# Two loads issued ahead of four stores, and ScalarE's order changed, in a chunked-attention and rational-MLP kernel

## The chip, the cores and the metric

The kernel runs as one program on one core of a Trainium2 chip. Its time is the device time of one execution in microseconds (us); of the kernel before it is the median of three executions. A profile of one more execution shows every instruction of the five engines: TensorE (PE, with its weight loads as PEld), VectorE (DVE), ScalarE (ACT), GpSimd (POOL) and SyncE (SP, which issues nearly all DMAs here). One DMA moves one block of a tensor between HBM and SBUF, and SP issues its DMAs one after the other.

## The reference

Attention over chunks of 64 rows, and then a two-layer MLP whose activation is a rational function (numpy, cut):

```python
scores = (1 / sqrt(64)) * q_c @ k_c.T          # per batch, head and chunk of 64 rows
attn = exp(scores - max); attn = attn / (sum(attn) + 1e-9)
x = (attn @ v_c) -> [4608 tokens, 512]         # heads side by side
h = x @ w_in                                   # 512 -> 2048
P = a[0] + a[1]*h + a[2]*h*h + a[3]*h*h*h
Q = 1 + |b[0]|*|h| + |b[1]|*h*h
out = (P / (Q + 1e-6)) @ w_out                 # 2048 -> 512, float32
```

## The kernel before

The 4608 tokens are 18 blocks of 256 (numbers 0 to 17). Each block has four steps s = 0 to 3, one for each 512 columns of the hidden layer. To keep float32 accuracy each operand of a matmul is split into a high part (`hi`, a cast) and a low part (`lo`, what the cast lost), and a product is three matmuls: hi*hi, hi*lo, lo*hi.

Every instruction is placed by hand. `START` lists the first 12 steps; after that `step(g)` walks a string of letters for each step, and each letter issues its instructions into the in-order queues of the engines. So the order of two letters matters only where they share an engine, or where they take a buffer from the same pool tag. The strings are `EARLY` (blocks 3 and 4), `STEADY` (blocks 5 to 16) and `LAST` (block 17). The letters that matter here, in block n:

- `F f` (PE): the hidden layer's matmuls into `ph`. `c a` (ACT): `C` and `A` read from `ph` (L402, L386). `Q p P` (DVE, L410, L422, L426), `b I J` (ACT, L391, L414, L418) and `g H R` (DVE, L431, L435, L439 in steps 0 and 1, L501, L505, L509 in steps 2 and 3) make the rational function. `Gp` (POOL, L444) makes its low part, in steps 0 and 1.
- `Z z y` (PE): the output matmuls of the step two before. For steps 2 and 3 of a block a seven-product scheme stands in their place, done in the next block: `V` (PE) in steps 0 and 1 and `V2` (PE) in step 1 add into `xacc` and `po`. Their sums are split by `hb` (ACT, L549, the high parts `shi`) and `lb` (DVE, L553, the low parts `slo`); `s0 h0 l0p` and `s2p h2 l2` do the same for the other sums, and `G2 L2` make the halves for step 2.
- `w o`: copy and add `xacc` and `po` into the output tile `o` (ACT L603, DVE L604 to L614); then `put` issues four stores (L675).
- `A S` (PE): the next block's attention output into `psx`, and the scores `pss` of the block after that from `q` and `k`. `X Y` split the attention output into `xhi` (ACT, L361) and `xlo` (DVE). `M U E0 E1`: maximum (DVE), scaling (DVE) and 16 exponentials (ACT, L304, in two halves). `n Np` normalise, `T` transposes on DVE (`et`, L322), `K` moves 16 sub-blocks by DMA (`at`, L330).
- `q k` (SP, L107): the loads of q and k for block n+2, 512 KB each. `q` takes a buffer of tag `xlo`, which the low sums also use; `k` takes one of tag `C`, the one that step 1's `C` has just left. `xhi`, `shi` and `o` share another tag, so `X` waits until the four stores of `o` have landed.
- `B1 B2 B3 D1 D2`: prepare a sum of weight blocks once (`tsum`, L477 to L495), in blocks 3, 4 and 5.

Tag `pa` holds one pair of PSUM banks: `pss` in step 3, then `xacc` of the next block. So `V` in step 0 can start only when `E1` has read `pss`.

Of the kernel before, what the change touches and what calls it, by code (L numbers as in the profile page):

```python
# [10 lines left out]
F32 = mybir.dt.float32  # L11
# [8 lines left out]
P = 128  # L20
UPB = 2
NB = 18
# [3 lines left out]
DM = 512  # L26
# [23 lines left out]
FIRST = 12  # L50
BY_PSUM = 3
CUT_FIRST, CUT_LAST = 24, 48
CUTS = {'y5': (48, 0), 'y4': (0, 0), 'y9': (48, 0)}

PIECES = [(m, fq, k) for m, fq in ((0, 0), (0, 1), (1, 0), (0, 2), (1, 1), (0, 3), (1, 2), (1, 3)) for k in (0, 1)]

# [2 lines left out]
def tile_chunked_attention_rational_moe(  # L59
# [13 lines left out]
    p2 = ctx.enter_context(tc.tile_pool(name="p2", bufs=2))  # L73
# [35 lines left out]
    def load_qk(n, early=False):  # L109
        if n >= QK_LATE:  # L110
            return
        if early:
            q, k = (p2.tile([P, W], F32, tag=t, name=f"{t}qk{n}") for t in "AB")
        else:
            qk = p2.tile([P, 2, W], F32, tag="raw", name=f"qk{n}", bufs=3)
            q, k = qk[:, 0, :], qk[:, 1, :]
        loaded["q", n], loaded["k", n] = q, k
        if not early:
            load_part(n, slice(0, W))
# [5 lines left out]
    def load_v(n):  # L125
        if n >= NB:
            return
        v = p2.tile([P, W], F32, tag="vt", name=f"v{n}", bufs=1)
        nc.sync.dma_start(out=v, in_=vP[n])
        loaded["v", n] = v  # L130
# [105 lines left out]
    def att_s(n, u=None, tag="pa"):  # L236
        before[0] += "S"
        pss = have("s", n, lambda: bank_pair(tag, f"pss{n}"))
        quarters(lambda g: slice(g * 64, g * 64 + 64), pss, loaded["q", n], loaded["k", n], u)
# [48 lines left out]
    def att_norm(n, u=None, engine=None):  # L288
        ec = by_group(exps(n, u))
        _, _, rs = stats(n, u)  # L290
        (engine or nc.vector).tensor_mul(ec, ec, spread(rs))
# [49 lines left out]
    def att_av(n, u=None, tag="pa"):  # L341
        before[0] += "X"
        psx = have("x", n, lambda: bank_pair(tag, f"psx{n}"))

        def cols(g):
            v, hp = divmod(g, NHP)
            return slice(hp * 128 + v * 64, hp * 128 + v * 64 + 64)

        quarters(cols, psx, loaded["v", n], att["at", n], u, n in turned)
# [100 lines left out]
    ST_FIRST = 5  # L450
    tw, xacc, wide = {}, {}, {}
    full, s_one, s_full, shi, slo = {}, {}, {}, {}, {}

    def whole(n):
        return ST_FIRST <= n < NB - 1

    def seven(n, s):
        return s >= 2 and whole(n)
# [2 lines left out]
        f = slice(FPS * (2 + k), FPS * (3 + k))  # L461
        return tuple(w[:, f, 256 * j:256 * j + 256] for w in (wo_hi, wo_lo))

    T_AT = {(3, 3): 0, (4, 1): 2, (4, 3): 1, (5, 1): 3}

    def t_terms(k):
        f32 = lambda z: tuple(w.bitcast(F32) for w in z)
# [73 lines left out]
    def s_hi(n, k):  # L541
        nc.scalar.copy(shi[n][0][:, k, :, :], s_one[n, 2 + k])
# [8 lines left out]
    def s_lo_pair(n, engine=None):  # L551
        slo[n][1] = p2.tile([P, 2, FPS, 128], F32R, tag="xlo", name=f"slo{n}_1")
        (engine or nc.vector).tensor_sub(slo[n][1], s_full.pop(n), shi[n][1].bitcast(F32))  # L553
# [58 lines left out]
    def s_out(n):  # L612
        o = wide.pop(n)
        nc.vector.tensor_add(o, o, obuf.pop(("late", n)))  # L614
        put(n, o)

    both = []

# [44 lines left out]
    def rows_out(n):  # L663

        return out[n * BT:(n + 1) * BT, :].rearrange("(u c t) f -> c u t f", u=UPB, c=2)

    def store(n):
        o = p2.tile([P, 2, DM], F32, tag="xhi" if n > 1 else "eo", name=f"o{n}")
        nc.scalar.copy(o, obuf.pop(n))
        put(n, o)  # L670

    def put(n, o):
        for c in range(2):
            for u in range(UPB):
                nc.sync.dma_start(out=rows_out(n)[c, u], in_=o[64 * u:64 * u + 64, c, :])  # L675
# [34 lines left out]
    def ph_tag(g):  # L710
        return "p1" if g == 1 or (g >= 10 and g % 2 == 0) else "p0"
# [45 lines left out]
    def run(program, then=""):  # L757
        words_ = [re.fullmatch(r"([A-Za-z]+)([0-9.]+)(?::(\w+))?", item).groups() for item in program.split()]
        letters = [name for name, _, _ in words_] + [then]
        for k, (name, args, tag) in enumerate(words_):  # L760
            ahead = next((x for x in letters[k + 1:] if x in ("F", "f", "Z", "z", "y", "r")), "")
            cuts[0] = CUTS.get(
                f"{name}{args}",
# [8 lines left out]
    one = lambda names, k: run(" ".join(f"{x}{k}" for x in names.split()))  # L772
    EARLY = (
# [4 lines left out]
    )  # L778
    STEADY = (
# [4 lines left out]
    )  # L784
    LAST = (
# [4 lines left out]
    )  # L790

    def step(g):
        n, s = steps[g]
        m = n + 1 if n + 1 < NB else None
        early = n + 2 if n + 2 < NB else None
        this, prev = whole(n), whole(n - 1)
        of_m = {
            "n": att_rs, "N": att_norm, "Np": lambda k: att_norm(k, engine=nc.gpsimd), "T": att_turn, "K": att_move, "X": att_xhi, "Y": att_xlo,
            "A": lambda k: (att_av(k, tag=ph_tag(g + 1)), load_v(k + 1)),
        }  # L800
        of_early = {"S": lambda k: (att_s(k), load_qk(k + 1)), "M": att_max, "U": att_sub,
                    "E0": lambda k: att_exp_half(k, 0), "E1": lambda k: att_exp_half(k, 1),
                    "q": lambda k: load_late("q", k), "k": lambda k: load_late("k", k)}
        pool = nc.gpsimd
        of_prev = {
            "G'": lambda k: chain_split(k, 3), "L'": lambda k: chain_rest(k, 3), "Lp'": lambda k: chain_rest(k, 3, pool),
            "s0": s_pair, "s0p": lambda k: s_pair(k, pool), "h0": lambda k: s_hi(k, 1), "l0": lambda k: s_lo(k, 1), "l0p": lambda k: s_lo(k, 1, pool),
            "hb": s_hi_pair, "lb": s_lo_pair, "lbp": lambda k: s_lo_pair(k, pool), "w": s_store, "o": s_out,
        }
        of_this = {  # L810
            "G2": lambda k: chain_split(k, 2), "L2": lambda k: chain_rest(k, 2), "L2p": lambda k: chain_rest(k, 2, pool),
            "s2": s_lone, "s2p": lambda k: s_lone(k, pool), "h2": lambda k: s_hi(k, 0), "l2": lambda k: s_lo(k, 0), "l2p": lambda k: s_lo(k, 0, pool),
        }
        other = {"g": chain_t, "H": chain_inv, "R": chain_g}
        orders = EARLY if n < ST_FIRST else LAST if n == NB - 1 else STEADY
        def later(f, *a, kind=""):
            todo.append((kind, lambda: f(*a)))

        for name in orders[s].split():
            if name.rstrip("p") in T_PARTS:  # L820
                if (n, s) in T_AT:
                    later(T_PARTS[name.rstrip("p")], T_AT[n, s], s, pool if name[-1] == "p" else nc.vector)
            elif name in of_m:
                if m is not None:
                    later(of_m[name], m)
            elif name in of_early:
                if early is not None:
                    later(of_early[name], early)
            elif name in of_prev:
                if prev:  # L830
                    later(of_prev[name], n - 1)
            elif name in of_this:
                if this:
                    later(of_this[name], n)
            elif name == "V":
                if not prev:
                    for x in "Zzy":
                        later(words, f"{x}{g - LAG}", kind="Z")
                    if s == 1:
                        later(store, n - 1)  # L840
                elif s == 0:
                    later(ff2_early, n - 1, kind="V")
                else:
                    later(ff2_late, n - 1, kind="V")
            elif name == "V2":
                if prev:
                    later(ff2_last, n - 1, kind="V")
            elif name == "y'":
                if prev:
                    later(words, f"y{g - 3}", kind="Z")  # L850
            elif name in "Zzy":
                later(words, f"{name}{g - LAG}", kind="Z")
            elif seven(n, s) and name in other:
                later(other[name], n, s)
            elif seven(n, s) and name in ("G", "Gp"):
                pass
            elif name == "Gp" and (g == FIRST or n == NB - 1):
                later(words, f"G{g}")
            else:
                later(words, f"{name}{g}", kind="F" if name in "Ff" else "")  # L860
# [8 lines left out]
    g = total  # L869
# [40 lines left out]
```

## Time and profile before

| | |
|---|---|
| median of three executions | 884.61 us (880.62, 885.65, 884.61) |
| profiled execution, its own time | 883.63 us |
| its span from first to last instruction | 881.7 us (1.93 us of its time lie outside) |
| PE busy | 842.9 us, 96% |
| DVE busy | 791.3 us, 90% |
| ACT busy | 591.5 us, 67% |
| POOL busy | 193.4 us, 22% |

Busy time is the time in which at least one instruction of that engine runs; a wait shows as idle time before an instruction, with what released it. A timeline row gives start and duration in us, engine, line, operation, output<-inputs, shape, and in brackets the idle time before it. SP has only issue times: its rows say when a DMA was issued and for how long the issue took, not when the data landed.

### The profile page before, as it was taken

What the parts mean: (1) busy time and instruction counts of PE and PEld (TensorE: products, weight loads), DVE (VectorE), ACT (ScalarE), POOL (GpSimd) and SP (SyncE); (2) the same over time, 40 slices, a digit from 0 to 9 for tenths busy, and PEclk for the clock granted to TensorE, in tenths of its full rate; (3) what the DMA queues carried; (4) which work ended last, traced back from release to release, by engine and by line L of the source; (5) the groups of instructions that cost most, each with busy time, mean ns of one, the idle gap of its engine ahead of it and who ended that gap; (6) DMA issues with size and microseconds to landing.
All of it is one profiled execution on the core that took longest, in us unless ns stands there. A gap on an engine that the chain in (4) does not pass through costs nothing.

```text
span 881.7 us, 21328 instructions
## 1 busy us (share of the span) xinstructions
PE 842.9 (96%) x9152; PEld 828.0 (94%) x9152; DVE 791.3 (90%) x736; ACT 591.5 (67%) x995; POOL 193.4 (22%) x99
## 2 busy tenths in 40 slices
PE   4999999999999899999999999999999999999997
PEld 3889999999999899999999999999999999899997
DVE  6999998978898989998999898999989898999996
ACT  5899865756575756668585848576766667585652
POOL 1222222015345221212122111212121212112200
PEclk9999999999999999999999999999999999999999
DMA  8753304020121203030302112030303030301010
GB/s 310 263 191 132 133 25 144 26 49 26 47 76 33 88 6 117 1 121 1 97 26 54 68 29 94 20 102 14 108 7 116 1 121 1 101 21 49 1 25 25
DMA packets 27422, 63.25 MB, mean 72 GB/s; under 512 B 6208, under 2 KB 13632, under 8 KB 25280
## 3 DMA queue, kind: packets, MB, share of 16 engines
q1 hardware_dynamic: 27088, 61.63, 21.6%
q8 instruction: 72, 1.18, 0.5%
q10 hardware_dynamic: 240, 0.26, 0.1%
q14 instruction: 22, 0.18, 0.1%
HBM read 45.09 MB, written 9.44 MB: 62 GB/s over the span
## 4 chain that ended last, share of the span: by engine, by line
PE 56%; DVE 18%; SPq 8%; ACT 7%; DMA 6%; issue 3%; POOL 1%; DVEq 0%; POOLq 0%; ACTq 0%
PE ph L382 27%; PE po L658 19%; SPq L330 6%; DMA k<-in_kT 5%; PE xacc L566 4%; DVE slo L553 4%; PE pss L219 2%; DVE B L435 2%; DVE B L410 2%; SPq L675 2%; DVE ghi L431 2%; ACT C L402 2%; ACT A L386 2%; DVE C L426 1%; DVE et L322 1%
## 5 line engine op out<-in xcount | busy, mean ns | idle before, releaser
L382 PE MATMUL ph<-xhi,wi_hi 128*128 128x256 f32 x1152 | 322.6, 280 | 0.8 <-DVE xlo L365 0.8
L382 PE MATMUL ph<-xlo,wi_hi 128*128 128x256 f32 x1152 | 319.7, 278 | 0.3 <-DVE xlo L365 0.3
L382 PE MATMUL ph<-xhi,wi_lo 128*128 128x256 f32 x1152 | 319.5, 277 | 0.0
L382 PEld LDWEIGHTS ph<-xhi,wi_hi 128*128 128x128 f32 x1152 | 216.5, 188 | 2.0 <-DVE xlo L365 1.0
L382 PEld LDWEIGHTS ph<-xlo,wi_hi 128*128 128x128 f32 x1152 | 216.9, 188 | 0.7 <-DVE xlo L365 0.6
L382 PEld LDWEIGHTS ph<-xhi,wi_lo 128*128 128x128 f32 x1152 | 217.0, 188 | 0.0
L444 POOL TENSOR_TENSOR glo<-B,A 128x1024 fp32r<-128x1024 f32 x38 | 96.5, 2540 | 335.1 <-DVE B L439 320.4
L658 PE MATMUL po<-wo_hi,ghi 128*128 128x256 f32 (+1 forms) x712 | 142.8, 281 | 0.4 <-DVE ghi L431 0.3
L658 PE MATMUL po<-wo_lo,ghi 128*128 128x256 f32 x712 | 141.0, 278 | 0.0
L402 ACT ACTIVATE C<-ph,ab 128x1024 f32<-128x1024 f32 x72 | 86.9, 1207 | 63.1 <-PE ph L382 63.1
L391 ACT ACTIVATE B<-B 128x1024 f32<-128x1024 f32 x60 | 63.8, 1063 | 84.0 <-DVE B L410 84.0
L658 PEld LDWEIGHTS po<-wo_hi,ghi 128*128 128x128 f32 x712 | 108.6, 189 | 1.5 <-DVE ghi L431 0.5
L658 PEld LDWEIGHTS po<-wo_lo,ghi 128*128 128x128 f32 x712 | 108.5, 189 | 0.0
L386 ACT ACTIVATE A<-ph,ab 128x1024 f32<-128x1024 f32 x72 | 80.0, 1112 | 39.9 <-PE ph L382 37.5
L426 DVE SCALAR_TENSOR_TENSOR C<-C,ab,ph 128x1024 f32<-128x1024 f32 x72 | 92.1, 1279 | 2.6 <-ACT B L394 0.7
L410 DVE SCALAR_TENSOR_TENSOR B<-A,ab,ph 128x1024 f32<-128x1024 f32 x60 | 75.8, 1264 | 16.3 <-ACT A L386 16.1
L658 PE MATMUL po<-wo_hi,glo 128*128 128x256 f32 (+1 forms) x712 | 90.3, 278 | 0.0
L422 DVE TENSOR_TENSOR C<-C,ph 128x1024 f32<-128x1024 f32 x72 | 87.4, 1213 | 0.6 <-ACT C L402 0.5
L414 ACT ACTIVATE A<-B,ab 128x1024 f32<-128x1024 f32 x72 | 83.0, 1153 | 7.1 <-DVE B L407 5.5
L658 PEld LDWEIGHTS po<-wo_hi,glo 128*128 128x128 f32 x712 | 85.5, 188 | 0.2
L418 ACT ACTIVATE A<-A,ab 128x1024 f32<-128x1024 f32 x72 | 83.1, 1155 | 2.1
L431 DVE SCALAR_TENSOR_TENSOR ghi<-C,ab,A 128x1024 fp32r<-128x1024 f32 x48 | 62.6, 1304 | 15.6 <-ACT A L418 14.2
(156 smaller groups left out, 1459.5 us busy)
## 6 DMA issues: line engine op xcount, KB each, us to landing
v<-in_vP SPq DMA_DIRECT2D x18, 512.0 KB, 3.6
out<-o SPq DMA_DIRECT2D x68, 128.0 KB, 2.4
raw<-in_w_in SPq DMA_DIRECT2D x8, 1024.0 KB, 6.7
raw<-in_w_out SPq DMA_DIRECT2D x8, 1024.0 KB, 4.8
at<-et SPq DMA_DIRECT2D x224, 32.0 KB, 1.9
k<-in_kT SPq DMA_DIRECT2D x12, 512.0 KB, 4.5
q<-in_qT SPq DMA_DIRECT2D x12, 512.0 KB, 4.0
qk<-in_qT SPq DMA_DIRECT2D x4, 512.0 KB, 4.8
```

Source lines behind the costliest of these rows:

```text
L382: nc.tensor.matmul(ph[:, fi, :], w[:, cc, f], x[:, cc, :], start=(k == 0), stop=(k == len(mm) - 1))
L386: nc.scalar.activation(ch[n, s][1], ch[n, s][0], AF.Abs, scale=b1a if n >= BY_PSUM else b0a)
L391: nc.scalar.activation(B, B, AF.Abs)
L402: nc.scalar.activation(ch[n, s][3], ch[n, s][0], AF.Identity, bias=k[2], scale=k[3])
L410: nc.vector.scalar_tensor_tensor(ch[n, s][2], A, b0a, h, ALU.add, ALU.mult)
L414: nc.scalar.activation(A, B, AF.Ln, bias=cst[:, 0:1], scale=2.0 ** -KLN)
L418: nc.scalar.activation(A, A, AF.Exp, bias=cst[:, 1:2], scale=-1.0)
L422: nc.vector.tensor_mul(C, C, h)
L426: nc.vector.scalar_tensor_tensor(C, C, coef(n, s)[1], h, ALU.add, ALU.mult)
L431: nc.vector.scalar_tensor_tensor(gbuf[n, s][0], C, a_of[0], A, ALU.add, ALU.mult)
L444: (engine or nc.vector).tensor_mul(gbuf[n, s][1], B, A)
L658: nc.tensor.matmul(acc(n, i, cols), g[:, fi, i * 128:(i + 1) * 128], w[:, FPS * s + fi, cols], start=start, stop=stop,)
```

## The change

The four stores leave the place where the output tile is made (`o`, and `store` for the early blocks) and become a letter of their own, `u`, which stands in step 2 behind `q` and `k`. In `STEADY` step 1 `hb` stands ahead of `a`. In step 3 `L2` goes from DVE to POOL (`L2p`), ahead of `s2p`; `h2` goes ahead of `E0`; `l2` goes behind `R`. Block 5 gets strings of its own (`FIFTH`); in its step 1 `B1` goes from POOL to DVE, ahead of `T`, and `B2` ahead of `p`. `CUTS` sets which output matmul pairs in the first 12 steps are split unevenly.

```diff
-CUTS = {'y5': (48, 0), 'y4': (0, 0), 'y9': (48, 0)}
+CUTS = {'y9': (28, 48)}
...
     def s_out(n):
         o = wide.pop(n)
         nc.vector.tensor_add(o, o, obuf.pop(("late", n)))
-        put(n, o)
+        wide[n] = o
+
+    def s_put(n):
+        put(n, wide.pop(n))
...
     def store(n):
-        o = p2.tile([P, 2, DM], F32, tag="xhi" if n > 1 else "eo", name=f"o{n}")
+        wide[n] = o = p2.tile([P, 2, DM], F32, tag="xhi" if n > 1 else "eo", name=f"o{n}")
         nc.scalar.copy(o, obuf.pop(n))
-        put(n, o)
+        if n < 2:
+            s_put(n)
...
     STEADY = (
...
-        "F f c a V hb lb V2 T B1p Q K w b p B2 o B3p P I J D1 g H R D2 Gp",
-        "F f Z c a z Q b I q J p P y g H R Gp k",
-        "F f A S a Q M X G2 Y Z b L2 c z U p s2p I J E0 P g H y h2 l2 R E1 Gp",
+        "F f c V hb a lb V2 T Q K w b p o P I J g H R Gp",
+        "F f Z c a z q Q b I k y u J p P g H R G",
+        "F f A S a Q M X G2 Y Z b L2p c z U p s2p I J h2 E0 P g H y R E1 l2 Gp",
...
+    FIFTH = (
...
+        "F f c a B1 V T K Q B2 b p B3p P I J D1 g H R Gp D2",
...
-        orders = EARLY if n < ST_FIRST else LAST if n == NB - 1 else STEADY
+        orders = EARLY if n < ST_FIRST else FIFTH if n == ST_FIRST else LAST if n == NB - 1 else STEADY
```

SP's queue, block 9 (steps 1 to 3), before (-) and after (+). `at10` are the 16 moves, `o8` the output of block 8, `q11` and `k11` the loads for block 11, `v11` that block's v.

```order
 L330 DMA at10_5751<-et10_5747 32x256 x16
-L675 DMA out_0<-o8_5768 64x512 x4
-L107 DMA q11_5879<-in_qT 128x1024
-L107 DMA k11_5903<-in_kT 128x1024
+L107 DMA q11_5871<-in_qT 128x1024
+L107 DMA k11_5877<-in_kT 128x1024
+L679 DMA out_0<-o8_5768 64x512 x4
 L129 DMA v11_5987<-in_vP 128x1024
```

The two loads now follow the 16 moves directly, and the four stores stand behind them.

ACT's queue, block 9, step 1. `shi8_1` are the high sums of block 8, `A9_1` is the first piece of the rational function of this step.

```order
 L418 ACTIVATE A9_0_5575<-A9_0_5575,ab_73 128x1024
 L402 ACTIVATE C9_1_5678<-ph9_1_5629,ab_73 128x1024
-L386 ACTIVATE A9_1_5680<-ph9_1_5629,ab_73 128x1024
-L549 CAST shi8_1_5718<-sf8_5578 128x1024
+L549 CAST shi8_1_5716<-sf8_5578 128x1024
+L386 ACTIVATE A9_1_5718<-ph9_1_5629,ab_73 128x1024
 L603 COPY o8_5768<-xacc8_5581 128x256
```

The cast of the sums and the making of `A` have changed places.

ACT's queue, block 9, the end of step 3. `e11` are the exponentials, `shi9_0` the high part of the lone sum, which POOL makes.

```order
 L418 ACTIVATE A9_3_6022<-A9_3_6022,ab_73 128x1024
-L304 ACTIVATE e11_6078,sm11_6026<-pss11_5989,sm11_6026 128x64 x8
-L542 CAST shi9_0_6074<-A9_2_5857 128x512
-L304 ACTIVATE e11_6078,sm11_6026<-pss11_5989,sm11_6026 128x64 x8
+L542 CAST shi9_0_6074<-A9_2_5853 128x512
+L304 ACTIVATE e11_6079,sm11_6026<-pss11_5989,sm11_6026 128x64 x16
 L402 ACTIVATE C10_0_6166<-ph10_0_6117,ab_73 128x1024
```

The cast now stands ahead of all 16 exponentials.

## Rows read from the trace of the kernel before

**Rows 1.** PE's waits, whole span: engine, line, waited for: us, times, longest.
```profile
PE pss L219 <- DMA k<-in_kT: 12.2, 9, 2.5
...
PE xacc L566 <- DVE slo L553: 5.1, 11, 0.5
...
PE pss L219 <- ACT ghi L518: 1.8, 1, 1.8
...
PE pss L219 <- ACT xhi L361: 1.2, 1, 1.2
```

**Rows 2.** Windows: stretch, engines' busy us (instructions), PE clock, DMA share, GB/s.
```profile
298.60:302.00 3.40, 3.40 (x54) 3.28 (x44) 2.77 (x4) 2.96 (x3) 0.64 (x1) 0.50 0.02 6
...
406.00:453.30 47.30, 45.41 (x505) 44.91 (x505) 43.13 (x42) 31.70 (x59) 9.26 (x5) 1.00 0.19 57
```

**Rows 3.** Timeline of SP, block 9, steps 1 and 2.
```profile
422.47 10.05 SPq L330 DMA_DIRECT2D at<-et  x16
432.64 3.38 SPq L675 DMA_DIRECT2D out<-o  x4
436.12 0.53 SPq L107 DMA_DIRECT2D q<-in_qT  x1
436.75 0.39 SPq L107 DMA_DIRECT2D k<-in_kT  x1
```

**Rows 4.** Timeline of PE, blocks 9 and 10: low sums, scores, next block's `V`.
```profile
421.09 0.39 PE L566 MATMUL xacc<-tt,slo 128*128 128x256 f32 x1 [0.46 <-DVE slo L553]
...
441.32 0.29 PE L219 MATMUL pss<-k,q 64*64 64x64 f32 x4 [1.43 <-DMA k<-in_kT]
...
453.47 0.28 PE L566 MATMUL xacc<-wo_hi,ghi 128*128 128x256 f32 x1
```

**Rows 5.** Timelines of DVE, ACT and POOL, block 9, step 1.
```profile
416.10 1.28 DVE L439 SCALAR_TENSOR_TENSOR B<-C,ab,B 128x1024 f32<-128x1024 f32 x1
418.01 3.03 DVE L553 TENSOR_TENSOR slo<-sf,shi 128x1024 fp32r<-128x1024 f32 x1 [0.63 <-ACT shi L549]
...
431.20 1.28 DVE L439 SCALAR_TENSOR_TENSOR B<-C,ab,B 128x1024 f32<-128x1024 f32 x1
...
415.88 1.11 ACT L386 ACTIVATE A<-ph,ab 128x1024 f32<-128x1024 f32 x1
416.88 1.04 ACT L549 CAST shi<-sf 128x1024 fp32r<-128x1024 f32 x1
...
417.55 2.40 POOL L444 TENSOR_TENSOR glo<-B,A 128x1024 fp32r<-128x1024 f32 x1 [5.12 <-DVE B L439]
```

**Rows 6.** Timelines of DVE and POOL, end of block 4.
```profile
263.47 1.22 DVE L495 TENSOR_TENSOR tt<-tsum,tt 128x1024 fp32r<-128x1024 f32 x1
...
263.72 3.23 POOL L444 TENSOR_TENSOR glo<-B,A 128x1024 fp32r<-128x1024 f32 x1 [5.20 <-DVE B L439]
```

**Rows 7.** Timeline of ACT, block 17, step 1.
```profile
838.10 1.06 ACT L549 CAST shi<-sf 128x1024 fp32r<-128x1024 f32 x1
```

**Rows 8.** Timelines of DVE and SP, block 5, steps 1 and 2.
```profile
275.66 1.24 DVE L322 STREAM_TRANSPOSE et<-e 128x1024 f32<-128x1024 f32 x1
...
279.11 2.40 SPq L675 DMA_DIRECT2D out<-o  x4
281.62 10.90 SPq L330 DMA_DIRECT2D at<-et  x16
...
293.18 0.43 SPq L107 DMA_DIRECT2D k<-in_kT  x1
```

**Rows 9.** Tile `o`, its 68 stores: from issue to landing.
```profile
DMA to landing us min/median/max: 2.2/2.4/4.0
```

**Rows 10.** Timelines of POOL and ACT, block 9, step 3.
```profile
441.12 1.28 POOL L531 TENSOR_TENSOR A<-B 128x512 f32<-128x512 f32 x1 [6.06 <-DVE B L509]
...
445.44 1.16 ACT L418 ACTIVATE A<-A,ab 128x1024 f32<-128x1024 f32 x1
...
451.55 0.28 ACT L304 ACTIVATION_READ_ACCUMULATOR e<-pss,sm 128x1 f32 x1
```

More of the change, by code (lines that the diff above doesn't have):

```diff
@@ L462, in b_block @@
         return tuple(w[:, f, 256 * j:256 * j + 256] for w in (wo_hi, wo_lo))
-    T_AT = {(3, 3): 0, (4, 1): 2, (4, 3): 1, (5, 1): 3}
+    T_AT = {(3, 3): 0, (4, 1): 2, (4, 3): 1} | {(5, s): 3 for s in range(2)}
     def t_terms(k):
@@ L774, in tile_chunked_attention_rational_moe @@
         "n Np F f c a Q b I p P V J g H R Gp",
[3 rows of a table removed]
[3 rows of a table added]
+    )
+    FIFTH = (
[4 rows of a table added]
     )
     STEADY = (
[4 rows of a table removed]
[4 rows of a table added]
     )
@@ L807, in step @@
             "s0": s_pair, "s0p": lambda k: s_pair(k, pool), "h0": lambda k: s_hi(k, 1), "l0": lambda k: s_lo(k, 1), "l0p": lambda k: s_lo(k, 1, pool),
-            "hb": s_hi_pair, "lb": s_lo_pair, "lbp": lambda k: s_lo_pair(k, pool), "w": s_store, "o": s_out,
+            "hb": s_hi_pair, "lb": s_lo_pair, "lbp": lambda k: s_lo_pair(k, pool), "w": s_store, "o": s_out, "u": s_put,
         }
@@ L829, in step @@
             elif name in of_prev:
-                if prev:
+                if prev or name == "u":
                     later(of_prev[name], n - 1)
```

13 rows, old and new, of tables (EARLY, FIFTH, LAST, STEADY) are left out of this document.

## The prediction

> **What bounds the kernel now.** I read the list of PE's waits first, since PE is busy 96% of the span. Between the first steps and the tail it waits at two places alone [rows 1]. One is the scores `pss`: nine waits booked on the load of k, 12.2 us in all. Two more, 1.8 and 1.2 us, are booked on ACT; they stand before the same instruction, in blocks like the others, so I count them as k's too, though that is read and not shown. The other is the low sums, `xacc<-tt,slo`: eleven waits, 5.1 us. Together 20.3 us.
>
> Then the windows. One steady block takes 47.30 us, of which PE is busy 45.41 and DVE 43.13 [rows 2]: PE sets the pace, DVE is close behind. PE's clock is granted in full in that block, but a stretch of 3.40 us in block 5 has it at 0.50, the 1.2 GHz level [rows 2]; PE stood idle for the longest wait of the list, 2.5 us [rows 1], just before it.
>
> Then the timelines of one block (9), to see what each wait hangs on. For k it is SP's queue: 16 moves of 0.63 us each end at 432.52, four stores follow until 436.02, then q, then k at 436.75 [rows 3]; PE, ready at 439.89, starts the scores at 441.32 [rows 4], 4.57 us behind k's issue. For the low sums it is DVE's L553, which takes 3.03 us [rows 5], where an instruction of the same kind and shape takes 1.22 [rows 6]. It starts 0.46 us after POOL's `glo`, and ends at 421.04, 1.09 us after POOL's end at 419.95 [rows 5]: DVE stood still until POOL was through. It started late because it waited 0.63 us for ACT's cast, which stood behind `A`.
>
> **The change part by part, in the times of block 9.**
>
> *`hb` ahead of `a`.* The cast takes the place of `A` at 415.88. It can't start much later: it also needs PE to have left the old `shi`, and in block 17, where the order is already the new one, the cast's row shows no wait before it [rows 7], and PE has no wait at the low sums there (eleven waits in twelve blocks). So it ends at 416.9 to 417.1, before L439's end at 417.38 [rows 5]; L553 can then follow L439 on its own engine with no wait between. POOL's `glo` waits for the same L439 and starts 0.17 us after its end. In block 4 the same race is seen with DVE first: L495 starts 0.25 us before POOL's `glo`, takes 1.22 us, and it is `glo` that stretches, to 3.23 [rows 6]. So L553 ends at about 418.6; PE wants it at 421.09 - 0.46 = 420.63 [rows 4]. The wait goes, with 2.0 us to spare: -5.1 us. `A` ends some 1.0 us later, near 418.2; who needs it, `Q`, stands on DVE behind L553 and the transpose, at 419.8, so that costs nothing. If L553 were late again, `A`'s delay would still be covered.
>
> The Trainium skill, page "SBUF — State Buffer", section "Who interferes with whom", gives the rule behind this: a DVE instruction with two SBUF inputs and a GpSimd instruction that reads SBUF shut each other out, and the one that issues second waits for all of the first. By that rule all hangs on 0.17 us, and the other order of start is my first rival below; the rows show both orders.
>
> *`q k` ahead of the stores.* L553's earlier end starts the transpose and the moves up to 2.4 us earlier: 422.47 becomes 420.1, and their end 430.1. q follows at once. k needs the buffer that L439 of step 1 leaves at 432.48 [rows 5], so it is issued by 432.6 even if DVE runs no earlier there, and lands 4.57 us later, at 437.2. PE wants it at 439.89 less the 0.46 saved before, 439.43. So the wait goes with 2.2 us to spare. If the moves start no earlier, q goes at 432.6 and k at 433.3, which lands at 437.8: still in time. An issue that hangs, as one of the four stores did here (3.38 us where block 5's four took 2.40 [rows 3, 8]), costs 1.0 and is covered. All k's waits: -(12.2 + 1.8 + 1.2) = -15.2 us.
>
> *What is behind the loads now.* The four stores are issued from 432.7 to 435.1, or 436.1 with one that hangs; the last then lands 2.4 us (median) to 4.0 (longest) after its issue [rows 9], from 434.5 + 2.4 = 436.9 to 435.5 + 4.0 = 439.5. `X` on ACT waits for that landing, and for PE's `psx`, which ends at 439.43. So it costs nothing to 0.1 us of ACT.
>
> *Block 5.* The transpose is through at 276.90, but the moves start at 281.62, behind the four stores of 279.11 [rows 8]; now they start at about 278.2, since `B1` goes ahead of the transpose and takes the 1.22 us of L495's kind [rows 6]. With 10.90 us they end at 289.1; k, which was issued at 293.18 [rows 8], goes at about 289.8, 3.4 us earlier, against a wait of 2.5 [rows 1]. So PE doesn't stand, and the stretch at half the clock, 3.40 us [rows 2], gives half of it back: -1.7 us.
>
> *Step 3.* On POOL `L2p` goes ahead of the lone sum, which takes 1.28 us at 441.12 [rows 10]. With one more such piece ahead the sum is ready by 444 to 445, before ACT is through with `J` at 446.60; so `h2` ahead of `E0` only changes places with eight exponentials, and `E1`, which ends at 451.83 [rows 10], ends no later for it. DVE has one instruction less. Nothing on PE's path: 0 (from -0.7 us a block for DVE's instruction, if DVE were the bound, to the third rival).
>
> *What is late next.* `V` needs the banks that `E1` leaves at 451.83. PE now comes to `V` at 453.47 [rows 4], and 0.46 + 1.43 = 1.89 us earlier in the new order, at 451.58. So ACT must get earlier by 0.25 us a block. It does: its chain runs from `V2` (0.46 earlier) over DVE's additions to `E1`, and DVE has 0.63 + (3.03 - 1.22) = 2.4 us more room before those additions. I take 0; if only half of what is missing were found, 11 x 0.13 = 1.4 us.
>
> *Blocks 3 and 4, the uneven pairs.* PE doesn't wait there, and the pairs move three splits of a matmul: 0, between -0.5 and +0.5 by the size of such pieces (a matmul of 0.28 to 0.39 us [rows 4]).
>
> **Sum.** -15.2 - 5.1 - 1.7 = -22.0 us. The profiled execution took 883.63 us, so 861.6; it lies 1.0 below the median, from which the sum is 862.6. I forecast 862.0.
>
> **Rivals.**
>
> *POOL first at L553.* If the cast ends after 417.5 in the steady blocks, POOL's `glo` is ahead again, and L553 ends at 421.04 as now. The 5.1 us stay, k's waits go all the same (above): 861.6 + 5.1 = 866.7. For it: a margin of 0.3 to 0.6 us. Against: L553 needs no new wait once the cast is done, and in block 4 DVE won by 0.25 us.
>
> *A new wait takes part.* `V` waits for `E1`, or `X` for the stores, by 0.25 to 1 us a block: 11 x 0.25 to 11 x 1.0 gives back 2.8 to 11 us: 864.4 to 873. For it: the 0.25 us above, and DVE at 91% of a block. Against: DVE's regained 2.4 us.
>
> *Slower: ACT stuck at `h2`.* ACT is in order, and `h2` now stands ahead of all exponentials. If POOL's two pieces end later than 446.60, ACT waits, and `E0`, `E1` and then PE's `V` with it. It eats what PE gains, 1.89 us a block, from an end of 448.5 on (with no slack at `V`); at 449.4 the kernel loses 0.9 x 11 = 10 us, some 894. For it: POOL stretches when DVE holds it off (3.23 against 2.40 us [rows 5, 6]). Against: two pieces of 1.3 us would need to be held off 4 us, and DVE works from PSUM then.
>
> *The fetch stays late.* If q and k hang on their buffers and not on the queue, only the low sums' 5.1 us go: 878.5. Against: DVE's L439 frees k's buffer 4.27 us before k is issued [rows 3, 5].
>
> **How the numbers follow.** Forecast 0.76 (its own range 860 to 865: the pairs, half a microsecond from either reading of the base, a small new wait); POOL first 0.11; a new wait 0.07; fetch late 0.03; slower 0.03. The range from 859.0 to 868.0 takes the first two, and the low part of the third. A change of 0.5%, 4.4 us, is about the least that a measurement of this kernel can tell from none. Faster by more: the first two cases, nearly all of the third, and the late fetch (0.7% below the median) but for a part, 0.95; within: 0.02; slower: 0.03.
>
> **What would show it.** In the changed profile PE's waits should have no `pss` on k and no `xacc` on `slo`; a steady block should take 45.4 us; L553 should take 1.22 us and the `glo` beside it 3.2; SP should issue q right behind the moves; PE's clock should be 1.0 in block 5. If L553 still takes 3.03, the first rival holds; if PE waits at `xacc` for ACT's exponentials, the second or third; if `pss` still waits, the fourth.

## The result, and the profile after

The changed kernel took 853.9 us (median of four, 851.6 to 855.4), the kernel before 883.2 us on the same chip (median of four): 0.9666 of before, 95% interval 0.9625 to 0.9708. The forecast was 862.0 (859 to 868). It is faster, as forecast, but by 29 us and not by 22; the time lies below the range.

PE's list of waits, of the changed kernel (columns as in [rows 1]):

```profile
PE pss L219 <- DVE sm L284: 4.9, 1, 4.9
PE pss L219 <- DMA Bqk<-in_kT: 4.7, 1, 4.7
PE psx L219 <- DMA v<-in_vP: 2.0, 1, 2.0
PE pst L317 <- DVE e L291: 1.0, 1, 1.0
PE po L661 <- issue: 0.5, 1, 0.5
```

No wait for k and none for the low sums is left; the first four rows belong to the first steps, and the last is a wait of 0.5 us that the kernel before does not have. So every wait that I wanted gone is gone, and yet the sum is too small. The page's busy line, of the changed kernel, and the chain's shares under it:

```profile
PE 834.8 (98%) x9152; PEld 823.6 (96%) x9152; DVE 769.4 (90%) x725; ACT 590.1 (69%) x995; POOL 216.2 (25%) x110
...
PE 96%; DMA 2%; DVE 1%; issue 0%; SPq 0%; DVEq 0%
```

PE runs the same 9152 matmuls, but its busy time fell by 8.1 us, from the 842.9 of the table before. The span less PE's busy time fell from 881.7 - 842.9 = 38.8 to 853.5 - 834.8 = 18.7, by 20.1. I had forecast 20.3 us of idle time, which came (20.1), and 1.7 us of busy time, where 8.1 came. The rest of this document is about those 6.4 us.

One steady block, a window of the changed kernel from one start of the scores to the next (eight blocks in a row take 44.76 us so; columns: stretch; its length; busy us of PE, PEld, DVE, ACT, POOL with instructions, those that reach over an edge included; PE clock, DMA share, GB/s):

```profile
385.37:430.13 44.76, 44.76 (x516) 44.56 (x510) 41.35 (x41) 31.57 (x60) 11.38 (x6) 1.00 0.20 60
```

A block's matmuls took 45.41 us of busy time before [rows 2], which I had taken for the least that a block could take. One block number has to be put right first: the timed rows that [rows 3, 4, 5, 10] and the prediction give to block 9 lie in block 8, whose step 1 starts its hidden-layer matmuls at 409.04 us in the kernel before, where block 9's step 1 starts them at 456.23. The steady blocks are alike, so nothing in the argument hangs on it. The same block, 8, in the changed kernel, DVE, ACT, POOL and SP (start, duration, idle before in brackets):

```profile
407.28 1.28 DVE L439 SCALAR_TENSOR_TENSOR B<-C,ab,B 128x1024 f32<-128x1024 f32 x1
408.49 1.22 DVE L553 TENSOR_TENSOR slo<-sf,shi 128x1024 fp32r<-128x1024 f32 x1
...
407.26 1.06 ACT L549 CAST shi<-sf 128x1024 fp32r<-128x1024 f32 x1
408.22 1.11 ACT L386 ACTIVATE A<-ph,ab 128x1024 f32<-128x1024 f32 x1
...
408.74 3.23 POOL L444 TENSOR_TENSOR glo<-B,A 128x1024 fp32r<-128x1024 f32 x1 [5.11 <-DVE B L439]
...
411.15 10.28 SPq L330 DMA_DIRECT2D at<-et  x16
421.53 0.52 SPq L107 DMA_DIRECT2D q<-in_qT  x1
422.15 0.38 SPq L107 DMA_DIRECT2D k<-in_kT  x1
422.62 2.75 SPq L679 DMA_DIRECT2D out<-o  x4
```

The cast is through at 408.32, before L439 ends; L553 starts 0.25 us ahead of POOL's `glo` and takes 1.22 us, and `glo` stretches to 3.23, as in [rows 6]; in [rows 5], with POOL first, it was L553 that took 3.03, and `glo` took 2.40. This is what the Trainium skill says on the page "SBUF — State Buffer", section "Who interferes with whom" (who issues first keeps the shared pair of ports for the whole instruction), and the trace agrees. The transpose and the moves follow, then q and k, then the stores.

### The profile page after: what moved, and what is told of

The parts are those of the page before. It is cut to its first block, busy times and chain, and to the rows that moved or that the text cites. A ratio compares the mean times of both kernels' runs of the same rounds, so it can differ in the third digit from the quotient of the medians.

```text
span 853.5 us, 21332 instructions
## 1 busy us (share of the span) xinstructions
PE 834.8 (98%) x9152; PEld 823.6 (96%) x9152; DVE 769.4 (90%) x725; ACT 590.1 (69%) x995; POOL 216.2 (25%) x110
## 4 chain that ended last, share of the span: by engine, by line
PE 96%; DMA 2%; DVE 1%; issue 0%; SPq 0%; DVEq 0%
PE ph L382 46%; PE po L661 29%; PE xacc L566 8%; PE po L566 6%; PE psx L219 2%; PE pss L219 2%; DMA v<-in_vP 1%; PE pe L661 1%; DMA raw<-in_w_in 1%; PE pl L199 1%; PE pe L699 1%; PE left L646 0%; PE pst L317 0%; DVE raw L181 0%; DVE raw L168 0%; PE po L650 0%
## 5 line engine op out<-in xcount | busy, mean ns | idle before, releaser
L444 POOL TENSOR_TENSOR glo<-B,A 128x1024 fp32r<-128x1024 f32 x38 | 106.6, 2805 | 305.1 <-DVE B L439 290.4
```

Source lines behind the costliest of these rows:

```text
L444: (engine or nc.vector).tensor_mul(gbuf[n, s][1], B, A)
```

## The experiments

Ratios are to the kernel before, which ran in turn with them on the same chip. The runs were made on several chips, on which the kernel before took 883.0 to 887.1 us; so times are compared by ratio, and spans only within one chip. Theory 1: a wait costs PE more than the idle bracket that the list of waits shows. Theory 2: the bracket is the whole price, and the missing 6 us came from another edit.

| kernel | ratio (95%) | PE busy | span less busy | waits over 0.15 us between the first steps and the tail: number, us |
|---|---|---|---|---|
| before | 1 | 842.9 | 38.8 | 23, 20.6 |
| changed | 0.9666 (0.9625 to 0.9708) | 834.8 | 18.7 | 1, 0.5 |
| changed, run again | 0.9636 (0.9611 to 0.9662) | 833.9 | 16.9 | 0, 0 |
| queue alone | 0.9761 (0.9729 to 0.9793) | 838.3 | 26.2 | 15, 8.2 |
| cast alone | 0.9720 (0.9690 to 0.9749) | 836.6 | 24.0 | 7, 5.4 |
| cast and queue | 0.9674 (0.9649 to 0.9699) | 833.9 | 20.3 | 4, 2.2 |
| changed, cast behind A | 0.9773 (0.9745 to 0.9801) | 839.1 | 25.0 | 13, 6.8 |
| changed, cast late | 0.9972 (0.9952 to 0.9992) | 845.5 | 37.6 | 13, 20.9 |
| changed, low sums late | 0.9791 (0.9767 to 0.9815) | 837.8 | 26.0 | 16, 8.2 |
| changed, stores first | 0.9686 (0.9656 to 0.9717) | 837.1 | 20.1 | 4, 3.0 |
| changed, old step 3 | 0.9647 (0.9624 to 0.9670) | 833.8 | 18.4 | 1, 0.2 |
| changed, old pairs | 0.9647 (0.9618 to 0.9675) | 833.4 | 17.6 | 1, 0.3 |

**One part alone: the queue.**

```diff
-        "F f Z c a z Q b I q J p P y g H R Gp k",
+        "F f Z c a z q Q b I k y u J p P g H R Gp",
```

(and the same in `EARLY` and `LAST`; the stores become `u`.)

> The kernel before with one part of the change: q and k ahead of the stores in every block, nothing else (no cast ahead of A, no orders of its own for block 5, old step 3, old cut). Theory 1 (a wait of PE costs more than the idle bracket that the list of waits shows: the time from start to start says 0.75 us a wait at the low sums where the bracket says 0.46, and about 1.75 a wait at the scores where the brackets say 1.38): all waits for k and the stretch at half clock go, the eleven waits at the low sums stay at 0.46; from start to start this part is worth 14.6 + 2.7 + 0.9 + 2.1 = 20 us, so 863. Theory 2 (the bracket is the whole price; the rest of the gain comes from some other part): 15.2 + 1.7 = 16.9 us, so 866.3. If the stores behind the loads hurt (they land 4.5 us after their issue in the changed kernel, 2.4 before): ACT's xhi waits for them and PE's psx with it, 870 or more.

Measured 0.9761, 21 us of 883. All waits for k went, but new ones came; its waits:

```profile
PE xacc L566 <- DVE slo L553: 2.6, 6, 0.5
PE pss L219 <- issue: 2.0, 4, 0.7
PE po L661 <- issue: 1.8, 2, 1.6
PE xacc L566 <- ACT e L304: 1.5, 2, 1.1
...
PE pss L219 <- ACT A L386: 0.3, 1, 0.3
```

Only 12.3 us of brackets went (20.56 to 8.24), and still the time fell by 21: nearer to theory 1, though neither foresaw the new waits. At the low sums six waits of eleven are left: in six blocks L553 now starts 0.67 to 1.02 us behind `glo` and takes 2.47 to 2.82 us, and only one of these waits; in the other five it takes 3.02, and each waits 0.46 us. `xacc` waiting for the exponentials is `V` behind `E1`, my second rival. It shows twice: 0.4 us at 488.6 us, and 1.1 us at 305.6, in block 6's step 0, before the first L553 (317.55), so a late L553 did not make that one. No PE wait shows that the stores behind the loads hurt.

**The other part alone: the cast.**

```diff
-        "F f c a V hb lb V2 T B1p Q K w b p B2 o B3p P I J D1 g H R D2 Gp",
+        "F f c V hb a lb V2 T B1p Q K w b p B2 o B3p P I J D1 g H R D2 Gp",
```

> The kernel before with one other part alone: the cast of the high sums ahead of A in the steady blocks' step 1. The eleven waits at the low sums go: 8.2 us by theory 1 (start to start), 5.1 by theory 2 (brackets). L553 at 1.22 us lets the moves start up to 2.4 us earlier, so k is issued about 2.4 us earlier even behind the four stores, lands near 438.9 in block 9's times against a need at 439.4: nearly all steady waits for k go too, block 5's 2.5 us and the stretch at half clock stay. Theory 1: 883.2 - 8.2 - 14 = 861; theory 2: 883.2 - 5.1 - 12.7 = 865.4. If the moves don't start earlier or the stores still hold k back: waits at the scores stay, 875 to 878.

Measured 0.9720, 24.7 us: by theory 1, 22; by theory 2, 17.8. Its waits, but for those of the first steps and the tail:

```profile
PE pss L219 <- DMA k<-in_kT: 2.5, 2, 1.5
...
PE pss L219 <- ACT ghi L518: 1.8, 1, 1.8
...
PE pss L219 <- issue: 0.3, 1, 0.3
```

Two waits of the nine booked on k are left, and one of the two that I had counted as k's, 1.8 us, though the stores stand ahead of k as before. So the late L553 made most of both waits: it held up the transpose and the moves, and these held up k. Each of the three has a place of its own. One (1.5 us at 297.0) is in block 5, where no L553 runs. One (1.0 us at 525.4) stands behind a k that landed 6.27 us after its issue, where the median is 4.6. The third stands in block 6, the one block of eleven where L553 still came behind POOL's `glo`, by 0.02 us, and took 3.48 us (the kernel with the cast alone):

```profile
320.40 3.48 DVE L553 TENSOR_TENSOR slo<-sf,shi 128x1024 fp32r<-128x1024 f32 x1 [0.19 <-ACT shi L549]
...
320.38 2.41 POOL L444 TENSOR_TENSOR glo<-B,A 128x1024 fp32r<-128x1024 f32 x1 [5.07 <-ACT shi L549]
...
344.47 0.29 PE L219 MATMUL pss<-k,q 64*64 64x64 f32 x5 [1.75 <-ACT ghi L518]
```

In the ten other blocks L553 starts 0.25 us ahead of `glo` and takes 1.22 us. This is the prediction's first rival, in one block of one run; the k wait came with it, which the rival had not expected.

**Both together, without block 5's orders, the new step 3 and the uneven pairs.** Both diffs above. Some smaller edits of the change, which the text on the change doesn't list, are left out too: new places of `a`, `B1`, `P` and `D2p` in `EARLY`, of `a` in `LAST`, and of `p` (behind `l0p b`) in `STEADY` step 0.

> The kernel before with two parts of the change together, the cast ahead of A and q and k ahead of the stores; without block 5's own orders, the new step 3, the uneven pairs. If these two are the whole of the gain between the first steps and the tail: no waits at the scores or the low sums, within 1 us of the changed kernel, and about 3 us better than the cast alone (0.972), which still waited 1.8, 1.5 and 1.0 us at the scores and had the stretch at half clock in block 5. If block 5's own orders or the new step 3 carry a part of the gain that my sum missed: 3 to 6 us slower than the changed kernel.

Measured 0.9674: these two lines are about nine tenths of the gain. What is left against the changed kernel, run on the same chip (856.2 to 852.6 us), is 3.6 us, as the second expectation had it. Both kernels issue their matmuls in the same order, so the starts can be compared one by one: between 286 and 316 us, around waits of 0.3, 0.6 and 0.7 us at 292, 294 and 307 us that the changed kernel lacks, this kernel loses 3.1 us; what it gains ahead of that (1.4) and loses behind it (1.5) about cancels. These 30 us are the end of block 5 and the start of block 6; old step 3 and old pairs, below, give nothing, so the orders of block 5 are the likely cause, though no run has them alone.

**The changed kernel with the cast behind A again.**

```diff
-        "F f c V hb a lb V2 T Q K w b p o P I J g H R Gp",
+        "F f c a V hb lb V2 T Q K w b p o P I J g H R Gp",
```

> The changed kernel with the cast of the high sums back behind A in the steady blocks' step 1, all else as changed. L553 is late again (3.03 us, behind POOL), eleven waits of about 0.46 us come back at the low sums, the scores still don't wait. Theory 1: 0.75 a block, 853.9 + 8.2 = 862.1; theory 2: 5.1, so 859.0. If the new step 3 or the other edits already move POOL out of the way: 854.

Measured 0.9773 (0.9745 to 0.9801), 9 to 12 us over the changed kernel by the ratios. Theory 1's 862.1 is 0.9761 of before and lies in that interval, theory 2's 859.0 (0.9726) does not. But it was not the eleven equal waits that made it: L553 takes 2.58 to 2.88 us in the first eight blocks and 3.02 in the last three; the waits at the low sums came back in seven blocks alone (2.2 us), five others stand at the scores, where I had expected none, and one of 1.1 us at `po`. PE's busy time is 4.3 to 5.2 us above that of the two profiles of the changed kernel.

**Two doses, to price a wait by itself.** In the first the cast stands behind A, Q and b, in the second the low sums stand behind Q:

```diff
-        "F f c V hb a lb V2 T Q K w b p o P I J g H R Gp",
+        "F f c V a Q b hb lb V2 T K w p o P I J g H R Gp",     # cast late
+        "F f c V hb a Q lb V2 T K w b p o P I J g H R Gp",     # low sums late
```

> A dose: the changed kernel with the cast of the high sums moved further back, behind A, Q and B's part in the steady blocks' step 1, so that PE waits longer at the low sums (1 to 4 us a block). What is measured is the price of a longer wait: theory 1 says the time rises over the changed kernel's by the sum of the idle brackets plus a fixed 0.25 to 0.3 us for each wait (11 waits: about 3 us more than the brackets); theory 2 says by the sum of the brackets alone. A third: later work makes part of a long wait good (PE is then followed by a slack elsewhere), and the time rises by less than the brackets.

> A second, smaller dose: the changed kernel with the low sums L553 behind Q on DVE, which waits for A. Eleven waits come at the low sums, I estimate 0.3 to 1.0 us each by the list of waits. Theory 1 (price of a wait is its bracket plus a fixed part, which was 0.3 to 0.4 us when the cast was late: brackets 19.8 us, time from start to start 24.6): time over the changed kernel is the brackets' sum plus 11 x 0.3 to 0.4, 3.3 to 4.4 us more than the brackets. Theory 2: the brackets' sum alone, 3 to 11 us. If L553 still comes in time: the changed kernel's time.

The low sums late, run on one chip with the changed kernel: 866.0 to 852.6 us, 13.4 more. The spans differ by 13.0, of which 9.1 is idle time of PE and 3.9 busy time. So theory 1 had it (3.3 to 4.4 over the brackets), and theory 2 falls: an edit that does nothing but make PE wait raises PE's busy time. For 16 waits (the eleven at the low sums and five others) it is 0.24 us each. One of them, PE in block 10 (the kernel with low sums late):

```profile
502.10 0.28 PE L566 MATMUL po<-wo_lo,shi 128*128 128x256 f32 x1
502.84 0.74 PE L566 MATMUL xacc<-tt,slo 128*128 128x256 f32 x4 [0.47 <-DVE slo L553]
503.42 0.67 PE L566 MATMUL po<-wo_hi,slo 128*128 128x256 f32 x5
```

and the same place in the changed kernel, run again:

```profile
499.10 0.28 PE L566 MATMUL po<-wo_lo,shi 128*128 128x256 f32 x1
499.21 0.62 PE L566 MATMUL xacc<-tt,slo 128*128 128x256 f32 x4
499.67 0.66 PE L566 MATMUL po<-wo_hi,slo 128*128 128x256 f32 x5
```

From the first row's start to the third's it is 1.32 us with the wait and 0.57 without: the wait costs 0.75, the bracket says 0.47. The first row shows most of the difference. It is booked as 0.28 us, but where nothing waits the next matmul starts 0.11 us after it: the last 0.17 us lie under the next matmul. Before a wait they lie under nothing, are booked as busy, and the bracket begins only behind them. The rest is in the second row: the four matmuls take 0.12 us more after the stop. The Trainium skill says why to be wary of that first row: page "Perfetto Trace Analysis", section "Tensor Engine Instruction (MATMUL, LD_WEIGHTS)", a TensorE instruction's end is estimated, from its size and a delay for SBUF, and not observed. The rows agree: 0.28 us is booked whether the next matmul starts 0.11 us later or 0.74.

The cast late gave 0.9972. Eleven waits of 1.6 to 1.8 us (19.8) were to cost 3 us more than their brackets; PE's busy time is 11.6 us above that of the changed kernel, run again (on another chip). Both theories were short. Two windows of that kernel, behind the stops of blocks 10 and 11, and rows of PE in block 10:

```profile
511.90:514.40 2.50, 2.50 (x14) 2.50 (x13) 1.25 (x1) 0.00 (x0) 0.00 (x0) 0.50 0.02 7
...
560.40:562.90 2.50, 2.50 (x24) 2.50 (x23) 1.91 (x3) 1.10 (x2) 0.00 (x0) 1.00 0.02 7
```

```profile
510.63 1.73 PE L566 MATMUL xacc<-tt,shi 128*128 128x256 f32 x8 [1.84 <-ACT shi L549]
512.16 0.41 PE L566 MATMUL po<-wo_hi,shi 128*128 128x256 f32 x1
512.37 0.41 PE L566 MATMUL po<-wo_lo,shi 128*128 128x256 f32 x1
```

After the wait of 1.84 us in block 10 the clock is granted at 0.50, the 1.2 GHz level, and matmuls follow one another at 0.21 us and not at 0.11. It is the same as in block 5 of before [rows 2], but not in every block: behind the wait of block 11, 1.84 us too, it stays at 1.00. The lower level stands in four stretches of 3.41 us (from 367.7, 415.5, 511.1 and 606.7 us), each behind one of the eleven stops, and costs half of each, 6.8 us; the mean granted clock of this run, 0.992, says the same. The other 4.8 us are 0.37 for each of 13 waits. Laid beside the changed kernel matmul by matmul, a stop of 1.84 us costs 2.1 to 2.2 us by the 60th matmul behind it where the clock stays, and 3.7 to 3.9 where it falls.

**The changed kernel with the stores ahead of the loads in the steady blocks.**

```diff
-        "F f Z c a z q Q b I k y u J p P g H R G",
+        "F f Z c a z u q Q b I k y J p P g H R G",
```

> The changed kernel with the steady blocks' stores ahead of q and k again; the cast stays ahead of A. Asks whether the order at SP's queue is still needed once the low sums are early. In the changed kernel's block 9 the moves end at 421.4 and four stores take 2.75 us, so q goes at 424.3, k at 424.9, and lands 4.4 to 5.6 us later, 429.3 to 430.5; the scores start at 430.1. Theory 1: no waits, or waits of up to 0.4 us by the list of waits, each with some 0.25 us more from start to start: 0 to 7 us slower than the changed kernel (0.964 to 0.972 of before). Theory 2: 0 to 4 us. If the queue's order is what makes the gain: all k's waits return, 875 or more.

Measured 0.9686, 856.0 us (854.3 to 859.0); the old pairs, on the same chip, took 852.7 (851.6 to 852.8). Of k's waits one came back, with three others under 0.7 us:

```profile
PE pss L219 <- DMA k<-in_kT: 1.3, 1, 1.3
PE pss L219 <- ACT A L386: 0.7, 1, 0.7
...
PE pss L219 <- issue: 0.6, 1, 0.6
```

So with the cast in its new place the order at SP's queue is worth about 3 us, not 15.

**Old step 3, and old pairs.**

```diff
-        "F f A S a Q M X G2 Y Z b L2p c z U p s2p I J h2 E0 P g H y R E1 l2 Gp",
+        "F f A S a Q M X G2 Y Z b L2 c z U p s2p I J E0 P g H y h2 l2 R E1 Gp",
```

```diff
-CUTS = {'y9': (28, 48)}
+CUTS = {'y5': (48, 0), 'y4': (0, 0), 'y9': (48, 0)}
```

> The changed kernel with step 3 as it was (DVE again makes the piece that POOL took over; h2 after H and y). The sum put this at nothing: within 0.1% of the changed kernel. If the relief of DVE (0.63 to 0.70 us a block) is what carries the missing 6 us: up to 11 x 0.5, 5 us slower.

> The changed kernel with the pairs of blocks 4 and 5 uneven as before (three entries for one). The sum put it at 0, between -0.5 and +0.5 us: same as the changed kernel, 0.963 to 0.967 of before. If the split changes who waits in the first steps: a wait of PE of 1 us or more before 300 us that the changed kernel doesn't have.

Both 0.9647, the changed kernel's own time (0.9636 and 0.9666): worth nothing, as the sum had it, and neither holds the missing 6 us.

## Why the prediction was wrong

The step that failed is the price of a wait. The sum took the idle brackets, 5.1 us at the low sums and 15.2 at the scores, for all that the stops cost, and a block's 45.41 us of busy time for its floor. The stops cost 8.2 and 17.3 us from start to start and 1.2 more in the matmuls behind them, and a block took 44.76. What was to go did go.

- **Low sums, -5.1 us.** The mechanism held to the instruction (cast early, L553 at 1.22, ahead of POOL by 0.25 us in all eleven blocks where the two meet, no wait). The size was off: the prediction priced eleven waits at their brackets. From start to start each took 0.75 us in the kernel before, so 8.2 us. Before's rows in block 10 show it as those above do:

```profile
515.13 0.28 PE L566 MATMUL po<-wo_lo,shi 128*128 128x256 f32 x1
515.87 0.74 PE L566 MATMUL xacc<-tt,slo 128*128 128x256 f32 x4 [0.46 <-DVE slo L553]
516.45 0.67 PE L566 MATMUL po<-wo_hi,slo 128*128 128x256 f32 x5
```

  A row that I passed over was nearer: the list of waits of the weight loads, of the kernel before, books 7.2 us for the same eleven stops.

```profile
PEld xacc L566 <- DVE slo L553: 7.2, 11, 0.7
```

- **k's waits, -15.2 us.** They went, all eleven, so the two booked on ACT were k's or came with them. Measured from the start of `psx` to the start of `pss`, the eleven places give 17.3 us; another 1.2 us lie in the matmuls that follow. The attribution was too narrow: I gave the whole term to SP's queue, and only asked whether it would still go if the moves started no earlier (it does: queue alone). The opposite question, what the cast alone does to k, was not asked; by itself it leaves three of these eleven waits, and two of 0.2 and 0.3 us.
- **Half clock in block 5, -1.7 us.** In the changed kernel `pss` and `po` there take 1.04 and 5.57 us from start to start, where they took 1.48 and 6.89: 1.76 us. That is the price in the profiled execution. Others of the kernel before show a lower mean clock: of 17 on one chip, the two at 1.000 took 883.4 us and the five at 0.989 to 0.991 took 887.9 to 892.0, while the changed kernel's executions lie at 0.998 to 1.000. So the lower level can cost the kernel before some 4 to 9 us (an estimate from these times), and a price read from one profile is a sample.
- **A steady block at 45.4 us.** This is the failed step in its plainest form: 47.30 less the idle time. It took 44.76. PE's busy time in a block was read as work, and 0.65 us of it belonged to the stops.
- **What is late next: nothing.** `V` found `E1` done, as forecast. That DVE's regained 1.8 us a block are the reason isn't shown: without them (queue alone) the wait is there once where the L553 of the block before was late, 0.4 us; the other, 1.1 us at the start of block 6, is back with cast and queue together, 0.7 us, and is gone with block 5's orders.
- **The stores behind the loads** land later than I said: in the changed kernel min, median and longest are below, against [rows 9]. It cost ACT 0.6 us in two places, and PE nothing.

```profile
DMA to landing us min/median/max: 2.2/4.5/6.6
```

- **Step 3, the pairs:** nothing, as forecast. Of the rivals none took place in the changed kernel; the first hung on a margin of 0.25 us, which held in all eleven blocks. With the cast alone it did not hold in one.

The sum with the right prices: 8.2 at the low sums, 17.3 at the scores, 1.8 for the clock, and 1.2 in other matmuls behind a stop make 28.5; the first steps lost about 0.5 in the profiled run (behind the wait of 2.0 us for `v`, most of which comes back later), and the tail behind the last matmul gave 0.2; the span fell by 28.2. The two kernels issue the same matmuls in the same order, so this can be followed one by one: from the scores at 249 us to the last matmul 28.1 of the 28.5 us are gained at the stops and within the 90 matmuls behind each, and no other matmul moves against its neighbour by more than 0.05 us. That leaves little room for a gain that doesn't go through a stop.

## What to carry to other kernels

Price a wait of TensorE from the start of the last matmul before it to the start of the first one behind it, less the spacing that this pair has where nothing waits; the idle bracket is a lower bound, here by 0.24 to 0.38 us a wait, and the busy time of a stretch with waits is no floor. Where two waits lie in one block, ask of each edit what it does to the other wait alone: here one late instruction of DVE had made most of both, and either edit by itself took about two thirds of the gain or more. A stop behind which the clock is granted at its lower level costs that stretch besides (1.8 us in block 5); it came behind four of eleven such stops in the kernel with the cast late, so it can't be read off the length of the stop alone.

## What the runs showed of the hardware

- A 128x256 matmul is booked at 0.28 us and follows its neighbour at 0.11 us. At the clock's lower level it is booked at 0.41 and follows at 0.21.
- With the cast late, the granted clock fell to 0.50 for 3.41 us behind four of the eleven stops of 1.6 to 1.8 us, and stayed at 1.00 behind the other seven. In the kernel before it fell behind the stop of 2.5 us and not behind another of 1.84 (488.9 us). After stops of 0.47 us it stayed at 1.00 in the kernel with the low sums late, whose mean clock is 1.000.
- Four 128 KB stores issued right behind two 512 KB loads land a median 4.5 us after issue, where they took 2.4 ahead of them. k landed 5.4 us after issue (median), before 4.5; but with the stores ahead of it again (stores first) it is 5.2, so the stores are not shown to be the reason.
- Where POOL's `glo` (2.4 us) was first, L553 ended 1.1 us behind `glo`'s end, whether it started 0.02 us after it (it took 3.48 us: cast alone, block 6), 0.46 (3.03: before) or 1.8 (1.67: low sums late). Where L553 was first by 0.25 us it took 1.22, and `glo` 3.23.
